# Block-sparse attention and two gated layers on one core: six weight pieces converted beside the first chunk's attention, small copies on GpSimd, loads for two groups

## The chip, the cores and the metric

One core of a Trainium2 chip runs the whole program. The time is the device time of one execution in microseconds; the median of several runs counts. The kernel before took 692.11 us (median of 3 runs, 690.9 to 693.22).

## What is computed

```python
def _attn_ref(q, k, v):                      # q, k, v: (2, 8, 768, 64) float32
    block, window = (32, 16)
    k_sum = k.reshape(B, H, nb, block, D).max(axis=3)
    v_sum = v.reshape(B, H, nb, block, D).mean(axis=3)
    scores_l = scale * np.matmul(q, k.transpose(0, 1, 3, 2))
    mask_l = np.abs(pos[:, None] - pos[None, :]) < window
    scores_s = scale * np.einsum('bhsd,bhnd->bhsn', q, k_sum) + np.log(block)
    scores_all = np.concatenate([np.where(mask_l, scores_l, -1e9), scores_s], axis=-1)
    a = softmax(scores_all)                  # with 1e-9 added to the sum
    return np.matmul(a, np.concatenate([v, v_sum], axis=2))

x = attention as (1536 tokens, 512)
x = ((x @ w_a) * (x @ w_b)) @ w_out          # 512 -> 1536 -> 512
h = x @ w_in                                 # 512 -> 2048
out = np.maximum(0.01 * h, h) @ w_out2       # 2048 -> 512
```

The weights come as float64. The kernel turns each into two float32r parts (high and low), does the same with activations, and makes each product from three float32r products.

## The kernel before

**Attention.** The 1536 tokens are cut into 3 chunks of 512. A chunk's attention is 8 groups; a group is one pair of heads and 256 queries in 4 windows of 64. In the first and third chunk two neighbouring groups share a head pair; in the second chunk, which lies across the two batches, no two do. For each group `load_q` (L130) and `load_vw` (L151) load queries and the windows of values, with one transfer for the queries and 4 to 6 for the windows; `q_prep` (L462) transposes queries on TensorE and ScalarE writes them, scaled, into a block-diagonal tile by four activations of 64x128 (L479, L480). `k_prep` (L436) transposes keys, takes the maximum over each 32 keys and copies the 24 block sums behind each window's keys (L455, on VectorE). `scores` (L483) multiplies, masks (L501, VectorE) and takes exponentials (L505, ScalarE). `normal` (L511) adds 1e-9 (L513) and takes the reciprocal (L514) on VectorE and multiplies on GpSimd (L515). `put_sums` (L181) copies the block sums of values into the group's window tile (L182, VectorE). `p_transpose` and `pv` finish the group; `pv` splits the result into two parts (L542, L543). `v_sums` (L390) adds values in blocks, mostly on GpSimd (L396).

**Weights.** 68 pieces of 512 KB are loaded by `stage` (L284, up to four ahead, three buffers) and converted by `convert` (L300) in seven steps: L316, L324, L329, L335, L341 and L349 on VectorE (the first, L316, together with L320 on ScalarE; L346 on ScalarE before L349). The results live in `W_EARLY` = 15 buffers, and in `W_LATE` = 9 more once the attention's memory is free, which is at the third chunk. The first chunk's products use 12 pieces, in the order a0 b0 a1 b1 a2 o0 b2 o1 a3 b3 o2 o3.

**Order.** `attention_ops` (L192) gives every step of group *i* a place 4*i* + offset; products (`PRODUCT`) are the steps with TensorE work. The first chunk's steps run in this order; after each product with a place over 9 (`PV`) one step of conversion is issued (`tick`, L360; L610), and at place 9 `first_weights` (L588) makes the first four pieces be converted if they aren't. `early` (L591) then feeds the first chunk's first four products (a0, b0, a1, b1) as its x tiles come. The later chunks' attention is cut into `micro` steps and issued between the matrix products of the chunk before at each call of `interleave` (L559), together with `pace["bg"]` = 3 steps of conversion. Then come the gated layer over 12 slices of 128 per chunk, in three rounds of four, and the second layer. All of this is the order of issue; the program's own scheduler, which works with a time model, then sets each engine's order and may pull a step forward into time that it holds to be idle. DMAs are all issued by SP.

Of the kernel before, what the change touches and what calls it, by code (L numbers as in the profile page):

```python
# [21 lines left out]
def kernel(  # L22
# [12 lines left out]
    nc = tc.nc  # L35
# [32 lines left out]
    W_EARLY, W_LATE = 15, 9  # L68
# [41 lines left out]
    vw_t = [keep.tile([P, 2, G, D], F32, tag=f"vw{i}", name=f"vw{i}") for i in range(2)]  # L110
# [9 lines left out]
    q_t, k_t, vb_t, vw_of = {}, {}, {}, {}  # L120
# [9 lines left out]
    def load_q(b, hp, g):  # L130
        t = q_p.tile([P, 2, GT // P, D], F32, tag="q", name="q")
        nc.sync.dma_start(
            out=t,
            in_=q[b, 2 * hp : 2 * hp + 2, g * GT : (g + 1) * GT].rearrange(
                "c (p n) d -> p c n d", p=P
            ),
        )
        q_t[b, hp, g] = t
# [12 lines left out]
    def load_vw(b, hp, g):  # L151

        t = vw_t[cnt["load"] % 2]
        cnt["load"] += 1

        def rows(o0, o1, w0, w1):
            if o0 < W < o1:
                rows(o0, W, w0, w1)
                rows(W, o1, w0, w1)
                return  # L160
            p0 = o0 + (KP if o0 >= W else 0)
            for c in range(2):
                src = v[b, 2 * hp + c, (g * G + w0) * W - WIN + o0, :]
                src = bass.AP(
                    tensor=src.tensor, offset=src.offset,
                    ap=[[D, o1 - o0], [W * D, w1 - w0], [1, D]],
                )
                nc.sync.dma_start(out=t[p0 : p0 + o1 - o0, c, w0:w1, :], in_=src)  # L168

        w0, w1 = int(g == 0), G - int(g == NGB - 1)  # L170
        if w0:
            rows(WIN, W, 0, 1)
        rows(0, W, w0, G)
        if w1 == G:
            rows(W, KL, 0, G)
        else:
            rows(W, W + WIN, 0, G)
            rows(W + WIN, KL, 0, w1)
        vw_of[b, hp, g] = t

    def put_sums(b, hp, g):  # L181
        nc.vector.tensor_copy(  # L182
            out=vw_of[b, hp, g][W : W + NB],
            in_=vs_t[b, 2 * hp // HV][:, 2 * hp % HV : 2 * hp % HV + 2, :]
            .unsqueeze(2)
            .to_broadcast([NB, 2, G, D]),
# [5 lines left out]
    def attention_ops():  # L192

        ops = []
        seen = set()
        for i, x in enumerate(sum(groups, [])):
            b, hp, g = x
            n = 4 * i

            def add(at, kind, f, *args):  # L200
                ops.append((n + at, kind, lambda: f(*args), i))
# [11 lines left out]
            add(-7, LOAD, load_q, *x)  # L213
# [3 lines left out]
            add(5, LOAD, load_vw, *x)  # L217
            add(7, SIDE, put_sums, *x)
# [217 lines left out]
    def k_prep(b, hp, g):  # L436
# [17 lines left out]
        if g == NGB - 1:  # L454
            nc.vector.tensor_copy(  # L455
# [6 lines left out]
    def q_prep(b, hp, g):  # L462
# [5 lines left out]
        for c in range(2):  # L468
            nc.tensor.transpose(
                ps[:, c * P : (c + 1) * P], q2[:, c].rearrange("p n d -> p (n d)"), ident  # L470
            )
        sc = -1.0 / math.sqrt(D)
        for c in range(2):

            dst = qbd[c * D : (c + 1) * D, :, c * W : (c + 1) * W].rearrange(
                "p w (o j) -> p w o j", j=2
            )
            src = ps[:, c * P : (c + 1) * P].rearrange("p (w o) -> p w o", w=G)
            nc.scalar.activation(out=dst[:, :, :, 0], in_=src[0:D], func=AF.Copy, scale=sc)  # L479
            nc.scalar.activation(out=dst[:, :, :, 1], in_=src[D:], func=AF.Copy, scale=sc)  # L480
# [30 lines left out]
    def normal(b, hp, g):  # L511
        pm, sm = st["pm", b, hp, g]
        nc.vector.tensor_scalar_add(sm, sm, 1.0e-9)  # L513
# [80 lines left out]

    n_first = len(groups[0])
# [6 lines left out]
    for i, x in enumerate(firsts):  # L602
        ops.append((PV, LOAD, lambda x=x: first_weights(*x), 0))
    ops.sort(key=lambda o: o[:2])
    rest = []
    for o in ops:
        if o[0] <= end or o[3] < n_first:
            o[2]()
            if o[1] == PRODUCT and o[0] > 0:
                tick(int(o[0] > PV))  # L610
# [82 lines left out]
    for n, (f, c) in enumerate(slices1):  # L693
        s, i = divmod(f, M1)
        if s == 0 and i == 0 and c + 1 < NC:
# [108 lines left out]
```

## Time and profile before

| | before |
|---|---|
| median of 3 runs | 692.11 us |
| the profiled execution | 693.21 us, its span 691.4 us |
| TensorE matmul busy | 650.4 us (94%) |
| VectorE busy | 421.7 us (61%) |
| ScalarE busy | 293.3 us (42%) |
| GpSimd busy | 50.7 us (7%) |
| mean granted TensorE clock | 0.968 |
| DMA | 53.43 MB, mean 77 GB/s |

A busy share is a mean over the span. The stages differ: attention fills the first 205 us or so, the matrix products the rest, so the shares are to be read stage by stage.

### The profile page before, as it was taken

How to read it: one execution, taken by the hardware profiler on the slowest of the kernel's cores; microseconds unless marked ns; L12 is line 12 of the kernel's file. 1: busy time of each engine (PE TensorE's matmuls, PEld its weight loads, DVE VectorE, ACT ScalarE, POOL GpSimd, SP SyncE). 2: the span in 40 equal slices, each digit the busy share in tenths (PEclk: the TensorE clock that was granted, in tenths of full speed). 3: DMA queues.
4: the chain of work that ended last, by engine and by line, in shares of the span. 5: the costliest groups of instructions: out<-in, count | busy, mean ns of one | idle time of the engine just before them, and what ended most of it. 6: DMA issues, size and time to landing. Idle time of an engine off the chain costs nothing.

```text
span 691.4 us, 9270 instructions
## 1 busy us (share of the span) xinstructions
PE 650.4 (94%) x3248; PEld 533.8 (77%) x3248; DVE 421.7 (61%) x978; ACT 293.3 (42%) x717; POOL 50.7 (7%) x79
## 2 busy tenths in 40 slices
PE   5697895999989999999999999999999999999997
PEld 4575784778768888888888888888888888888886
DVE  4999999443329999679924299943239432322423
ACT  6786566574545544244412255522235332222221
POOL 7324200110110000000000000000000000000000
PEclk9898997699989999999999999999999999999999
DMA  7976356220103444314410024210002000010101
GB/s 170 268 212 182 96 151 173 49 66 20 26 19 123 126 153 136 104 62 127 147 32 0 1 91 145 70 61 1 0 1 92 0 1 0 15 48 0 62 0 62
DMA packets 66862, 53.43 MB, mean 77 GB/s; under 512 B 34304, under 2 KB 60928, under 8 KB 66816
## 3 DMA queue, kind: packets, MB, share of 16 engines
q1 hardware_dynamic: 66816, 52.84, 25.6%
q8 instruction: 26, 0.43, 0.2%
q14 instruction: 20, 0.16, 0.1%
HBM read 49.68 MB, written 3.15 MB: 76 GB/s over the span
## 4 chain that ended last, share of the span: by engine, by line
PE 85%; DVE 8%; DMA 2%; SPq 2%; ACT 1%; issue 1%; DVEq 0%
PE ps_c L550 33%; PE ps_t L550 21%; PE ps_a L550 13%; PE ps_b L550 13%; PE ps_t L488 3%; DVE pm L501 1%; PE ps_t L534 1%; DMA vb<-in_v_dram 1%; DVE wc L335 1%; PE ps_t L523 1%; SPq L168 1%; ACT pm L505 1%; DVE vw L182 1%; DMA wst<-in_moe_w_a_dram 1%; DVE wc L324 1%
## 5 line engine op out<-in xcount | busy, mean ns | idle before, releaser
L550 PE MATMUL ps_c<-wsp,gs 128*128 128x512 f32 x576 | 139.6, 389 | 0.0
L550 PEld LDWEIGHTS ps_c<-wsp,gs 128*128 128x128 f32 x576 | 108.1, 188 | 22.5
L550 PE MATMUL ps_c<-gs,wsp 128*128 128x512 f32 x432 | 106.8, 392 | 0.0
L550 PEld LDWEIGHTS ps_c<-gs,wsp 128*128 128x128 f32 x432 | 80.3, 188 | 16.4
L550 PE MATMUL ps_t<-x,wsp 128*128 128x512 f32 x336 | 80.1, 394 | 0.0
L550 PEld LDWEIGHTS ps_t<-x,wsp 128*128 128x128 f32 x336 | 63.7, 190 | 13.4
L550 PE MATMUL ps_t<-ys,wsp 128*128 128x512 f32 x288 | 72.1, 389 | 0.0
L550 PE MATMUL ps_a<-x,wsp 128*128 128x512 f32 x252 | 69.7, 408 | 0.4 <-ACT x L542 0.2
L550 PE MATMUL ps_b<-x,wsp 128*128 128x512 f32 x252 | 66.5, 397 | 0.0
L550 PEld LDWEIGHTS ps_t<-ys,wsp 128*128 128x128 f32 x288 | 54.1, 188 | 11.2
L320 ACT ACTIVATE wc<-wst 128x512 f32<-128x512 f32 x68 | 46.0, 678 | 37.8 <-DVE wsp L349 37.2
L759 DVE SCALAR_TENSOR_TENSOR h<-h,ps_t 128x512 f32<-128x512 f32 x24 | 16.5, 686 | 67.6 <-ACT h L758 67.6
L550 PEld LDWEIGHTS ps_a<-x,wsp 128*128 128x128 f32 x252 | 47.3, 193 | 10.9 <-ACT x L542 1.7
L550 PEld LDWEIGHTS ps_b<-x,wsp 128*128 128x128 f32 x252 | 47.9, 191 | 9.5
L346 ACT CAST wsp<-wc 128x512 fp32r<-128x512 f32 x68 | 42.2, 622 | 29.4 <-DVE wc L341 27.6
L349 DVE TENSOR_TENSOR wsp<-wc,wsp 128x512 fp32r<-128x512 f32 x68 | 47.5, 699 | 10.5 <-ACT wsp L346 10.4
L335 DVE SCALAR_TENSOR_TENSOR wc<-wst,wc 128x512 int32<-128x512 int32 x68 | 48.9, 720 | 0.4
L341 DVE CUSTOM_DVE_ANT_0 wc<-wc,wr 128x1024 uint16<-128x1024 uint16 x68 | 48.5, 714 | 0.5
L505 ACT ACTIVATE pm<-pm,nb 128x128 f32<-128x128 f32 x96 | 37.7, 395 | 25.2 <-DVE nb L501 25.1
L571 DVE TENSOR_TENSOR gs<-h,gs 128x512 fp32r<-128x512 f32 x48 | 33.2, 691 | 24.7 <-ACT gs L570 24.5
L758 ACT COPY h<-ps_t 128x512 f32<-128x512 f32 x24 | 14.1, 587 | 72.4 <-PE ps_t L550 72.4
L570 ACT CAST gs<-h 128x512 fp32r<-128x512 f32 x48 | 29.8, 621 | 32.5 <-DVE h L759 29.4
(112 smaller groups left out, 800.9 us busy)
## 6 DMA issues: line engine op xcount, KB each, us to landing
wst<-in_moe_w_out_dram SPq DMA_DIRECT2D x28, 512.0 KB, 3.2
wst<-in_moe_w_in_dram SPq DMA_DIRECT2D x16, 512.0 KB, 3.7
wst<-in_moe_w_a_dram SPq DMA_DIRECT2D x12, 512.0 KB, 4.0
wst<-in_moe_w_b_dram SPq DMA_DIRECT2D x12, 512.0 KB, 3.9
k<-in_k_dram SPq DMA_DIRECT2D x16, 192.0 KB, 3.3
q<-in_q_dram SPq DMA_DIRECT2D x24, 128.0 KB, 2.8
vb<-in_v_dram SPq DMA_DIRECT2D x8, 384.0 KB, 5.5
out_dram<-acc SPq DMA_DIRECT2D x12, 256.0 KB, 2.1
```

The costliest lines, as they stand in the source:

```text
L320: nc.scalar.activation(out=t["c"].bitcast(F32), in_=hi_w.bitcast(F32), func=AF.Abs)
L335: nc.vector.scalar_tensor_tensor(out=t["c"], in0=hi_w, scalar=-0x40000000, in1=t["c"], op0=ALU.bitwise_and, op1=ALU.bitwise_or,)
L341: nc.vector.tensor_tensor(out=t["c"], in0=t["c"], in1=t["r"], op=ALU.add)
L346: nc.scalar.copy(out=t["w"][:, 0], in_=t["c"].bitcast(F32))
L349: nc.vector.tensor_tensor(out=t["w"][:, 1], in0=t["c"].bitcast(F32), in1=t["w"][:, 0].bitcast(F32), op=ALU.subtract,)
L488: nc.tensor.matmul(out=ps[:, w, :], lhsT=qbd[:, w, :], rhs=kts[:, (g * G + w) * SC : (g * G + w) * SC + P], start=True, stop=True,)
L505: nc.scalar.activation(out=pm[:, w, :], in_=pm[:, w, :], func=AF.Exp, scale=-1.0, bias=nb[:, w : w + 1], accum_out=sm[:, w : w + 1],)
L550: nc.tensor.matmul(out=ps, lhsT=w(a), rhs=x(b), start=first and j == 0, stop=last and j == 2)
L570: nc.scalar.copy(out=t[:, 0], in_=src)
L571: nc.vector.tensor_tensor(out=t[:, 1], in0=src, in1=t[:, 0].bitcast(F32), op=ALU.subtract)
L758: nc.scalar.copy(out=h, in_=ps)
L759: nc.vector.scalar_tensor_tensor(out=h, in0=h, scalar=0.01, in1=ps, op0=ALU.mult, op1=ALU.max)
```

## The change

Conversion: `W_EARLY` 14 and `W_LATE` 10. While the first chunk's attention is issued, two steps of conversion follow each product from the first on, until six pieces are begun; `first_weights` moves four places later. `pace["bg"]` is 4 in the first chunk, 1 in the second, 3 in the third, and 1.4 from the second round on. Loads: `load_q`, `load_vw` and `put_sums` work for *n* groups, two where the next group has the same heads and chunk; window tiles are twice as large, query tiles have two buffers for two groups each. Queries are laid out as keys are, so the block-diagonal tile takes two activations of 64x256 in place of four of 64x128. GpSimd takes the copies of block sums (L182, L455) and the addition of 1e-9 (L513).

```diff
-    W_EARLY, W_LATE = 15, 9
+    W_EARLY, W_LATE = 14, 10
-    vw_t = [keep.tile([P, 2, G, D], F32, tag=f"vw{i}", name=f"vw{i}") for i in range(2)]
+    vw_t = [keep.tile([P, 2, GC * G, D], F32, tag=f"vw{i}", name=f"vw{i}") for i in range(2)]
...
-    def load_q(b, hp, g):
-        t = q_p.tile([P, 2, GT // P, D], F32, tag="q", name="q")
-        nc.sync.dma_start(
-            out=t,
-            in_=q[b, 2 * hp : 2 * hp + 2, g * GT : (g + 1) * GT].rearrange(
-                "c (p n) d -> p c n d", p=P
-            ),
-        )
-        q_t[b, hp, g] = t
+    def load_q(b, hp, g, n):
+
+        t = q_p.tile([P, GC * GT // P, 2, D], F32, tag="q", name="q", bufs=2)
+        for c in range(2):
+            nc.sync.dma_start(
+                out=t[:, 0 : n * GT // P, c, :],
+                in_=q[b, 2 * hp + c, g * GT : (g + n) * GT].rearrange("(n p) d -> p n d", p=P),
+            )
+        for i in range(n):
+            q_t[b, hp, g + i] = t[:, i * GT // P : (i + 1) * GT // P]
...
-    def load_vw(b, hp, g):
+    def load_vw(b, hp, g, n):
...
+        nw = n * G
...
-        w0, w1 = int(g == 0), G - int(g == NGB - 1)
+        w0, w1 = int(g == 0), nw - int(g + n == NGB)
...
-    def put_sums(b, hp, g):
-        nc.vector.tensor_copy(
-            out=vw_of[b, hp, g][W : W + NB],
+    def put_sums(b, hp, g, n):
+        nc.gpsimd.tensor_copy(
+            out=vw_run[b, hp, g][W : W + NB],
...
-            .to_broadcast([NB, 2, G, D]),
+            .to_broadcast([NB, 2, n * G, D]),
...
-            add(-7, LOAD, load_q, *x)
...
-            add(5, LOAD, load_vw, *x)
-            add(7, SIDE, put_sums, *x)
+            run = (b, hp, g - 1) == prev
+            if not run:
+
+                n = 1 + int((b, hp, g + 1) in groups[i // len(groups[0])])
+                add(-7, LOAD, load_q, *x, n)
+                add(5, LOAD, load_vw, *x, n)
+                add(7, SIDE, put_sums, *x, n)
+            prev = x
...
-            nc.vector.tensor_copy(
+            nc.gpsimd.tensor_copy(
                 out=kts[:, 0:NW, W : W + NB],
...
         for c in range(2):
-            nc.tensor.transpose(
-                ps[:, c * P : (c + 1) * P], q2[:, c].rearrange("p n d -> p (n d)"), ident
-            )
...
-            nc.scalar.activation(out=dst[:, :, :, 0], in_=src[0:D], func=AF.Copy, scale=sc)
-            nc.scalar.activation(out=dst[:, :, :, 1], in_=src[D:], func=AF.Copy, scale=sc)
+
+            nc.scalar.activation(
+                out=qbd[c * D : (c + 1) * D, :, c * W : (c + 1) * W],
+                in_=ps[c * D : (c + 1) * D, :GT].rearrange("p (w o) -> p w o", w=G),
+                func=AF.Copy, scale=-1.0 / math.sqrt(D),
+            )
...
-        nc.vector.tensor_scalar_add(sm, sm, 1.0e-9)
+        nc.gpsimd.tensor_scalar_add(sm, sm, 1.0e-9)
...
+    N_FIRST = 6
...
-        ops.append((PV, LOAD, lambda x=x: first_weights(*x), 0))
+        ops.append((PV + 4, LOAD, lambda x=x: first_weights(*x), 0))
...
-            if o[1] == PRODUCT and o[0] > 0:
-                tick(int(o[0] > PV))
+            if o[1] == PRODUCT and o[0] > 0 and (bg or cnt["conv"] < N_FIRST):
+                tick(2)
...
         s, i = divmod(f, M1)
+        if i == 0:
+            pace["bg"] = {(0, 0): 4, (0, 1): 1, (0, 2): 3}.get((s, c), 1.4)
```

## Rows read from the trace of the kernel before

**Rows 1.** Stages: busy us (instructions) per engine, granted clock, DMA share, GB/s.

```profile
0.00:20.00 20.00, 11.85 (x55) 10.26 (x56) 9.72 (x48) 12.21 (x47) 13.31 (x48) 1.00 0.75 189
20.00:120.00 100.00, 77.25 (x531) 61.00 (x532) 96.86 (x275) 69.95 (x233) 25.80 (x20) 0.88 0.64 178
120.00:147.00 27.00, 24.20 (x178) 18.85 (x176) 12.48 (x57) 17.54 (x70) 5.18 (x5) 0.76 0.22 54
147.00:205.00 58.00, 54.31 (x366) 44.37 (x365) 20.02 (x84) 27.13 (x94) 6.40 (x7) 0.94 0.12 29
205.00:691.00 486.00, 482.78 (x2130) 399.37 (x2128) 282.64 (x514) 166.48 (x276) 0.00 (x0) 1.00 0.18 59
```

**Rows 2.** The page's slices: VectorE's busy tenths in 40 equal slices.

```profile
DVE  4999999443329999679924299943239432322423
```

**Rows 3.** Chain of waits, around 50 us: start, length, what.

```profile
50.39 1.66 DVE wc L335
52.05 1.15 DVE sm L513
```

**Rows 4.** Timeline of GpSimd at the same time: start, length, instruction.

```profile
50.04 3.13 POOL L396 TENSOR_TENSOR vb<-vb,vb 96x512 f32<-96x512 f32 x2
```

**Rows 5.** The three moved lines, whole run: ns min/median/max, first and last start.

```profile
L182 DVE COPY vw<-vs x24: 410/419/1372, 18.7 to 194.2; 24x512 f32<-24x512 f32 x24
L455 DVE COPY kts<-ks x8: 297/366/1369, 6.9 to 124.1; 128x288 f32<-128x288 f32 x8
L513 DVE TENSOR_SCALAR sm<-sm x24: 148/168/1225, 15.6 to 195.5; 128x4 f32<-128x4 f32 x24
```

**Rows 6.** VectorE's lines from 205 us on: count, busy us, mean ns, idle before.

```profile
L335 DVE SCALAR_TENSOR_TENSOR wc<-wst,wc 128x512 int32<-128x512 int32 x51 | 34.9, 686 | 0.2
L329 DVE TENSOR_SCALAR wc<-wc 128x512 int32<-128x512 int32 x51 | 21.5, 421 | 0.1
```

**Rows 7.** VectorE's lines from 20 to 120 us, same columns.

```profile
L335 DVE SCALAR_TENSOR_TENSOR wc<-wst,wc 128x512 int32<-128x512 int32 x17 | 14.0, 823 | 0.2
L341 DVE CUSTOM_DVE_ANT_0 wc<-wc,wr 128x1024 uint16<-128x1024 uint16 x17 | 13.6, 798 | 0.1
L349 DVE TENSOR_TENSOR wsp<-wc,wsp 128x512 fp32r<-128x512 f32 x15 | 11.2, 746 | 0.4 <-ACT wsp L346 0.4
L329 DVE TENSOR_SCALAR wc<-wc 128x512 int32<-128x512 int32 x17 | 8.4, 492 | 0.0
L316 DVE TENSOR_SCALAR wr<-wst 128x512 int32<-128x512 uint32 x19 | 7.9, 417 | 1.0 <-DMA wst<-in_moe_w_a_dram 0.9
...
L324 DVE TENSOR_SCALAR wc<-wc 128x512 f32<-128x512 f32 x17 | 7.8, 456 | 0.0
L182 DVE COPY vw<-vs 24x512 f32<-24x512 f32 x10 | 5.8, 587 | 0.5 <-PE ps_c L534 0.2
...
L513 DVE TENSOR_SCALAR sm<-sm 128x4 f32<-128x4 f32 x11 | 3.9, 352 | 0.0
...
L455 DVE COPY kts<-ks 128x288 f32<-128x288 f32 x5 | 3.4, 681 | 0.0
```

**Rows 8.** GpSimd: two lines over the run (min/median/max ns), one instruction by time.

```profile
L226 POOL MEMSET vw<- x2: 524/524/525, 0.7 to 1.2; 128x512 f32 x2
...
L515 POOL TENSOR_TENSOR pm<-pm,sm x24: 1038/1040/1307, 16.3 to 196.1; 128x512 f32<-128x512 f32 x24
...
8.84 0.11 POOL L256 MEMSET negm_last<- 128x16 f32 x1
```

**Rows 9.** Chain of waits at the first conversion.

```profile
16.18 4.28 DMA wst<-in_moe_w_a_dram
```

**Rows 10.** Chain of waits at the end of the third chunk's attention.

```profile
197.94 1.64 DMA vw<-in_v_dram
```

**Rows 11.** DMA issues over the run: count, KB each, median us to landing.

```profile
k<-in_k_dram SPq DMA_DIRECT2D x16, 192.0 KB, 3.3
q<-in_q_dram SPq DMA_DIRECT2D x24, 128.0 KB, 2.8
```

More of the change, by code (lines that the diff above doesn't have):

```diff
@@ L119 @@
     pace = {"micro": 0.0, "bg": 3}
-    q_t, k_t, vb_t, vw_of = {}, {}, {}, {}
+    q_t, k_t, vb_t, vw_of, vw_run = {}, {}, {}, {}, {}
     def load_k(b, hp):
@@ L168, in rows @@
                 nc.sync.dma_start(out=t[p0 : p0 + o1 - o0, c, w0:w1, :], in_=src)
-        w0, w1 = int(g == 0), G - int(g == NGB - 1)
+        w0, w1 = int(g == 0), nw - int(g + n == NGB)
         if w0:
             rows(WIN, W, 0, 1)
-        rows(0, W, w0, G)
-        if w1 == G:
-            rows(W, KL, 0, G)
+        rows(0, W, w0, nw)
+        if w1 == nw:
+            rows(W, KL, 0, nw)
         else:
-            rows(W, W + WIN, 0, G)
+            rows(W, W + WIN, 0, nw)
             rows(W + WIN, KL, 0, w1)
-        vw_of[b, hp, g] = t
-    def put_sums(b, hp, g):
-        nc.vector.tensor_copy(
-            out=vw_of[b, hp, g][W : W + NB],
+        for i in range(n):
+            vw_of[b, hp, g + i] = t[:, :, i * G : (i + 1) * G, :]
+        vw_run[b, hp, g] = t[:, :, 0:nw, :]
+    def put_sums(b, hp, g, n):
+        nc.gpsimd.tensor_copy(
+            out=vw_run[b, hp, g][W : W + NB],
             in_=vs_t[b, 2 * hp // HV][:, 2 * hp % HV : 2 * hp % HV + 2, :]
             .unsqueeze(2)
-            .to_broadcast([NB, 2, G, D]),
+            .to_broadcast([NB, 2, n * G, D]),
         )
@@ L195, in attention_ops @@
         seen = set()
+        prev = None
         for i, x in enumerate(sum(groups, [])):
             b, hp, g = x
-            n = 4 * i
             def add(at, kind, f, *args):
-                ops.append((n + at, kind, lambda: f(*args), i))
+                ops.append((4 * i + at, kind, lambda: f(*args), i))
             vi, r = divmod(2 * hp, HV)
@@ L467, in q_prep @@
         ps = at_bank()
+        for i in range(GT // P):
+            nc.tensor.transpose(
+                ps[:, i * P : (i + 1) * P], q2[:, i].rearrange("p c d -> p (c d)"), ident
+            )
         for c in range(2):
-            nc.tensor.transpose(
-                ps[:, c * P : (c + 1) * P], q2[:, c].rearrange("p n d -> p (n d)"), ident
-            )
[L472 to L476, printed above, removed]
-            )
-            src = ps[:, c * P : (c + 1) * P].rearrange("p (w o) -> p w o", w=G)
-            nc.scalar.activation(out=dst[:, :, :, 0], in_=src[0:D], func=AF.Copy, scale=sc)
-            nc.scalar.activation(out=dst[:, :, :, 1], in_=src[D:], func=AF.Copy, scale=sc)
+            nc.scalar.activation(
+                out=qbd[c * D : (c + 1) * D, :, c * W : (c + 1) * W],
+                in_=ps[c * D : (c + 1) * D, :GT].rearrange("p (w o) -> p w o", w=G),
+                func=AF.Copy, scale=-1.0 / math.sqrt(D),
+            )
         st["qk", b, hp, g] = qbd
```

## The prediction

> **What bounds the kernel now.** I read the views from coarse to fine. The page's engine table puts TensorE at 94% of the span and so says little. Cutting the span into stages [rows 1] says more: from 205 us on TensorE is busy for 482.8 of 486 us at a granted clock of 1.00 (the 2.4 GHz level), all of it expert matrix products that the change doesn't touch. Nothing is to be had there; what the change can win or lose lies in the first 205 us, and shifts the rest as a block.
>
> In those 205 us there are three stretches. In the first 20 us VectorE is busy for 9.72 us only. From 20 to 120 us it is busy for 96.86 of 100 us, while TensorE has 77.25, ScalarE 69.95 and the DMA engines 64% [rows 1]; the row of VectorE's slices shows the same block of nines [rows 2]. This is a VectorE-bound stretch: first-chunk attention, weight conversion and half of the second chunk's attention share one engine. From 120 to 205 us TensorE is nearly full again (24.20 of 27 and 54.31 of 58 us), but at mean clocks of 0.76 and 0.94, so the clock stood at its 1.2 GHz level for part of them.
>
> Inside the VectorE stretch the chain of waits shows a second thing: instructions that take much longer than they should. A 128x4 addition stands there with 1.15 us and a join of weights with 1.66 us [rows 3], while GpSimd runs two additions from 50.04 to 53.17 us [rows 4]. The usual times are 168 ns for that addition [rows 5] and 686 ns for that join [rows 6]. So a GpSimd instruction holds up VectorE instructions that work in SBUF.
>
> **The change part by part.** All sums go against the profiled execution, 693.2 us (span 691.4 and 1.8 around it); it lies 1.1 us above the median of 692.1.
>
> *Three kinds of small instructions leave VectorE for GpSimd.* In the stretch they are 10 copies of value sums (L182, 5.8 us), 11 additions of 1e-9 (L513, 3.9) and 5 copies of key sums (L455, 3.4) [rows 7]. At their undisturbed medians of 419, 168 and 366 ns [rows 5] that is 4.2 + 1.85 + 1.8 = 7.9 us of work; the other 5.3 us were waiting for GpSimd, and will fall on the next SBUF instruction instead. So 7.9 us leave VectorE. What comes back is the hold-up by the new GpSimd work. Its price per us: in the stretch five of the conversion's six instructions are longer than in the GpSimd-free part after 205 us [rows 6, 7] (L341 and L349 differ from L335, and L324 from L329, by under 1 ns there): 17 x 137, 17 x 112, 15 x 60, 17 x 71 and 17 x 35 ns, 6.9 us; with the 5.3 above 12.2 us, for 25.8 us of GpSimd [rows 1], 0.47 us per us.
>
> No row shows GpSimd doing such copies. Its clear of 128x512 takes 524 ns and its two-input product of 128x512 takes 1040 [rows 8]; a copy reads one stream, so I take the middle, 0.75 us for 512 columns (ends 0.52 and 1.04) and 1.5 us for the 1024 of two groups. In the stretch that makes about three double copies and three single ones (6.8 us), five key copies of 288 columns (about 0.45 each, 2.2), and eleven tiny additions, for which the 0.11 us clear of 16 columns [rows 8] is nearest (0.15 each, 1.6): 10.6 us, ends 7.3 and 15. At 0.47 this returns 5.0 us. Net **-2.9 us**; ends -7.9 (no hold-up) and +7.1 (15 us, all of it held up).
>
> *A rule of the Trainium skill speaks against this part.* What the rows show is above: 1.15 us for a 168 ns addition under a GpSimd instruction [rows 3, 5]. The Trainium skill, "GPSIMD Engine Reference", Key points, says that GpSimd shares its SBUF interfaces with VectorE and contends with VectorE instructions in a two-port mode or with two SBUF inputs; the trace agrees, with 1.15 us for 0.168. Its section Engine selection has one-input GpSimd work at roughly line rate; by the page's 1.2 GHz a double copy would be about 0.85 us (an estimate), and the net of this part nearer -5.
>
> *Fewer conversions in the stretch.* The early pool goes from 15 to 14 pieces, and 15 conversions finish in the stretch [rows 7]. One conversion is 417 + 456 + 492 + 823 + 798 + 746 ns = 3.7 us of VectorE [rows 7]. That one piece moves past 205 us, where VectorE has 203 us free [rows 1]: **-3.7 us**. Two further pieces have five of their six steps in the stretch although their room comes later (17 against 15 in [rows 7]); the program's scheduler pulls them forward into what it thinks is idle time. I leave them where they are (0; -6 if they now stay out).
>
> *Conversion starts earlier.* Ticks now run from the first products on instead of from the first group's P.V product. Before, the first weight's transfer takes 4.28 us from 16.18 us on and VectorE waits for it [rows 9]. Moved ahead, three 512 KB transfers pass the first value windows and keys on SP's queue. Those have some us of slack, since VectorE, not they, is late afterwards; the DMA engines are at 75% in the first 20 us [rows 1]. VectorE idles for 10.3 of these 20 us; about one piece should fit: **-4 us** (0 to -7).
>
> *Key-sum copy behind the masks.* The first such copy starts at 6.9 us on VectorE [rows 5]. On GpSimd it queues behind the mask set-up, whose last instruction starts at 8.84 [rows 8], and the first scores and exponentials wait for it: **+1.5 us** (0 to +2). Later normalisations and copies stand in one GpSimd queue too; a product that waits for a reciprocal holds the copies behind it, which is in the ends above.
>
> *Loads for two groups.* They halve the value-window transfers in the first and third chunk and make buffers free sooner. At the end of the third chunk's attention there is a wait of this kind: the last group's window lands until 199.6 us [rows 10], since its buffer comes free only when the group two before it is done. TensorE idles 3.7 us in that stage and its clock of 0.94 over 58 us costs up to 3.5 more [rows 1]. I take **-4 us** (0 to -7). Queries now come in 256-byte runs, as the keys already do; 192 KB of keys land 3.3 us after issue and 128 KB of queries after 2.8 [rows 11], so I price that at nothing. Two activations of twice the columns in place of four relieve ScalarE, which isn't the bound: nothing, as long as VectorE covers it.
>
> *Clock.* If TensorE is starved less before 120 us, part of the 0.76 in the 27 us behind it (6.5 us) comes back: **-2 us** (0 to -6).
>
> *Pace later.* 1.4 steps at each of some six interleave points per slice is 8.4 steps, 1.2 pieces per slice, against 12 pieces for 12 slices. Enough, and VectorE has room: nothing. If a piece came late, TensorE would wait for about one conversion, 3.7 us.
>
> Sum: -2.9 - 3.7 - 4 + 1.5 - 4 - 2 = -15.1. 693.2 - 15.1 = 678.1, and against the median 1.1 less: **677 us**.
>
> **The rivals.** *Slower, by the shared port.* GpSimd instructions cost their upper ends (15 us more in the stretch) and each of their microseconds stops VectorE, since this engine is always in an SBUF instruction there: +15 - 7.9 = +7.1; the earlier weights compete with keys and values and give nothing, +2 at the start, -3.7 for the piece, 0 in the third chunk: +5.4, about 697. It decides where hold-up per us times new GpSimd time passes 11.6 us. For it: [rows 3]. Against it: at the measured 0.47 it would need 25 us of new GpSimd time.
>
> *The wait moves to the weights.* Only six of the twelve pieces that the first chunk's products use are ready when its attention ends. At one piece per 6.7 us (15 in 100 us, [rows 7]) the twelfth came at about 100 us; if attention ends near 66 us and the six others keep that rhythm, it comes at 106, and TensorE stands in front of the products. That eats -2.9, -3.7, -4 and the clock; the third chunk's -4 and +1.5 remain: 690. For it: by the same rhythm the kernel before had eight pieces at 77 us, six are fewer. Against it: VectorE has less else to do then.
>
> *More than that.* Pieces 13 and 14 and the two begun ones really move to 120 us and later, where VectorE is busy for 12.48 of 27 and 20.02 of 58 us [rows 1]: 2 x 3.7 + 2 x 3.0 = 13.4 more, and 2 of clock: 662.
>
> *Not what it says.* The scheduler may pull the seventh and later conversions beside the first chunk anyway, as it did with pieces 16 and 17. Then VectorE's sum stays as I have it, and so does the time; it is part of the forecast.
>
> **How the numbers follow.** Forecast (668 to 686) 0.45; more (662) 0.17; weights late (690) 0.20; port (697) 0.18. A measurement of this kernel tells about 0.3%, 2.1 us, from no change. Faster by that, below 690.0: 0.45 + 0.17 + half of 0.20, 0.72; the other half within it, with a little of the port case, 0.12; slower 0.16. For 8 in 10 I reach from 661 to 695: this leaves the far half of the large gain and the far half of the port case outside.
>
> **What would show it.** Right: the end of the VectorE block at 105 to 110 us in place of 120, no idle TensorE before the last P.V product of the third chunk, and everything after it moved as a block. The port shows as conversions and additions stretched to a GpSimd instruction's end, and as GpSimd copies of over 1 us. Late weights show as TensorE waiting for a conversion's last subtraction before the first chunk's third or fourth slice. Wrong altogether if TensorE idles after 205 us.

## The result, and the profile after

The kernel after took 701.6 us (median of 4 runs) beside 692.04 us for the kernel before: a ratio of 1.0134 [1.0093, 1.0175]. It is slower, where 677 us and a gain had been forecast, and it lies outside the range given. The profiled execution took 703.6 us, its span 701.5.

The stages of the kernel after, with the columns of [rows 1] (busy us and instructions of TensorE, its weight loads, VectorE, ScalarE, GpSimd; granted clock, DMA share, GB/s):

```profile
0.00:20.00 20.00, 11.32 (x50) 9.60 (x50) 10.36 (x48) 10.71 (x38) 15.05 (x50) 1.00 0.96 233
20.00:120.00 100.00, 75.94 (x463) 60.05 (x462) 83.11 (x212) 56.66 (x178) 43.01 (x43) 0.85 0.57 153
120.00:147.00 27.00, 20.03 (x153) 15.63 (x151) 9.80 (x46) 14.67 (x57) 6.15 (x11) 0.75 0.29 65
147.00:205.00 58.00, 54.09 (x383) 43.48 (x378) 18.29 (x88) 31.75 (x107) 14.70 (x22) 1.00 0.19 43
205.00:230.00 25.00, 23.56 (x149) 19.04 (x148) 16.19 (x40) 12.73 (x29) 1.93 (x3) 1.00 0.19 61
230.00:701.00 471.00, 467.84 (x2064) 387.20 (x2062) 271.99 (x493) 159.01 (x263) 0.00 (x0) 1.00 0.18 59
```

From 230 us on the matrix products run as before, at 1.00 and 99% busy, so the loss lies ahead of them. In the 20 to 120 us stretch VectorE is busy for 83.11 us in place of 96.86 [rows 1]: it did get the relief that the change was to bring, and more of it (13.8 us) than the prediction's sum has for this stretch (2.9, 3.7 and 4). TensorE has not gained from it (75.94 against 77.25 us busy). GpSimd went from 25.80 to 43.01 us.

VectorE's slices show where the relief went; the row answers to [rows 2]:

```profile
DVE  4799993332337999759984187983239532232423
```

The block of nines is shorter: it ends at the sixth slice, near 105 us, where before it reached the seventh, near 120. That was forecast as the sign of success, and here it is no success: the attention results come later. ScalarE copies each group's P.V result out of PSUM, so its eighth copy marks the end of the first chunk's attention, its 24th the end of all attention:

| | eighth result, us | 24th result, us | span, us | conversions finished before the eighth |
|---|---|---|---|---|
| before | 69.1 | 200.4 | 691.4 | 6 |
| after | 87.7 | 212.1 | 701.5 | 12 |

The row of that eighth copy after (start, length, what):

```profile
87.74 0.35 ACT L549 CAST x<-ps_c 128x256 fp32r<-128x256 f32 x1
```

18.6 us are lost by then; 5.8 come back in the second chunk, for which only two of the 14 early conversions are left, and 1.1 in the third. That the conversions are the reason isn't shown: e13 below, with seven left, makes up as much there. In both kernels the span ends 489 to 491 us after the 24th result. So a late eighth result is not lost time one for one; the ratios decide.

### The profile page after: what moved, and what is told of

It is laid out like the page before. It is cut to its first block, busy times and chain, and to the rows that moved or that the text cites. A ratio compares the mean times of both kernels' runs of the same rounds, so it can differ in the third digit from the quotient of the medians.

```text
span 701.5 us, 9146 instructions
## 1 busy us (share of the span) xinstructions
PE 652.8 (93%) x3248; PEld 535.0 (76%) x3248; DVE 409.7 (58%) x922; ACT 285.5 (41%) x669; POOL 80.8 (12%) x127
## 4 chain that ended last, share of the span: by engine, by line
PE 84%; DVE 6%; ACT 4%; issue 2%; POOL 2%; DMA 1%; SPq 1%; POOLq 0%; ACTq 0%; DVEq 0%
PE ps_c L557 33%; PE ps_t L557 20%; PE ps_a L557 13%; PE ps_b L557 13%; PE ps_t L495 3%; ACT pm L512 2%; PE ps_t L530 1%; DVE pm L508 1%; PE ps_t L541 1%; DMA vb<-in_v_dram 1%; POOL pm L522 1%; DVE wc L333 1%; DVE wc L344 1%; DVE v L415 1%; DVE wsp L358 1%
## 5 line engine op out<-in xcount | busy, mean ns | idle before, releaser
L557 PEld LDWEIGHTS ps_c<-wsp,gs 128*128 128x128 f32 x576 | 108.2, 188 | 22.4
L557 PEld LDWEIGHTS ps_c<-gs,wsp 128*128 128x128 f32 x432 | 80.7, 188 | 16.6
L358 DVE TENSOR_TENSOR wsp<-wc,wsp 128x512 fp32r<-128x512 f32 x68 | 50.1, 741 | 13.2 <-ACT wsp L355 13.1
L350 DVE CUSTOM_DVE_ANT_0 wc<-wc,wr 128x1024 uint16<-128x1024 uint16 x68 | 48.7, 720 | 0.4
```

Of the source, the lines that this page charges most:

```text
L350: nc.vector.tensor_tensor(out=t["c"], in0=t["c"], in1=t["r"], op=ALU.add)
L358: nc.vector.tensor_tensor(out=t["w"][:, 1], in0=t["c"].bitcast(F32), in1=t["w"][:, 0].bitcast(F32), op=ALU.subtract,)
L557: nc.tensor.matmul(out=ps, lhsT=w(a), rhs=x(b), start=first and j == 0, stop=last and j == 2)
```

## The experiments

Ratios are to the kernel before, run beside each kernel. `issue_after(x)` in a diff sets an instruction behind x in its own engine's order and adds no other wait. "V" stands for the value-sum copies (L182 before, L186 after), "K" for the key-sum copies (L455, L464), "A" for the additions of 1e-9 (L513, L520).

### One part undone, or one part alone

**e1: the kernel after with V, K and A back on VectorE.**

```diff
-        nc.gpsimd.tensor_copy(
+        nc.vector.tensor_copy(
             out=vw_run[b, hp, g][W : W + NB],
...
-            nc.gpsimd.tensor_copy(
+            nc.vector.tensor_copy(
                 out=kts[:, 0:NW, W : W + NB],
...
-        nc.gpsimd.tensor_scalar_add(sm, sm, 1.0e-9)
+        nc.vector.tensor_scalar_add(sm, sm, 1.0e-9)
```

> The changed kernel with its three moves to GpSimd undone (both copies of sums and the addition of 1e-9 back on VectorE); conversion, pace and loads stay changed. Theory F (the fill): with slower steps on GpSimd the program's scheduler holds VectorE to be idle in the first chunk's attention and fills it with conversions pulled forward; in VectorE's order 12 of 14 conversions stand before the eighth group's result in the changed kernel, 7 of 15 in the one before, 8 of 14 in this one. At 3.7 us each that is four less than in the changed kernel, 15 us at the first chunk's end, about half of it left at the end: 690 to 694, the eighth result near 72 us. Theory P (the port): only the hold-up by GpSimd goes, about 3 us: 698. Theory L (the loads of two groups and the early weights crowd the first 20 us of DMA): 700.

Measured 0.9951 [0.9924, 0.9977]; eighth result at 69.5 us.

**e2: the kernel after with the conversion's old places and pace.**

```diff
-            if o[1] == PRODUCT and o[0] > 0 and (bg or cnt["conv"] < N_FIRST):
-                tick(2)
+            if o[1] == PRODUCT and o[0] > 0:
+                tick(int(o[0] > PV))
...
-        ops.append((PV + 4, LOAD, lambda x=x: first_weights(*x), 0))
+        ops.append((PV, LOAD, lambda x=x: first_weights(*x), 0))
...
-            pace["bg"] = {(0, 0): 4, (0, 1): 1, (0, 2): 3}.get((s, c), 1.4)
+            pace["bg"] = 3
```

> The changed kernel with the pace of conversion as before (one step per product behind the ninth place, first weights at the ninth place, three steps per interleave point); GpSimd moves and loads stay changed. Theory C (the new pace, two steps from the first product on, is what brings conversions in front of attention): back to 692. Theory F: in VectorE's order 11 conversions still stand before the eighth result, so the pace is not the cause: 698 to 702. Theory P: 701.

Measured 1.009 [1.0062, 1.0118]; eighth result at 87.3 us, ten conversions before it.

**e3: the kernel after with loads and value sums for one group.**

```diff
-            run = (b, hp, g - 1) == prev
+            run = False
...
-                n = 1 + int((b, hp, g + 1) in groups[i // len(groups[0])])
+                n = 1
```

> The changed kernel, but loads and copies of value sums for one group each (window and query tiles keep their new size). Theory L: back to 692 to 694. Theory F: 10 conversions in place of 12 stand before the eighth result: 695 to 699. Theory P: as many microseconds on GpSimd or a little more: 701 to 703.

Measured 1.0082 [1.0049, 1.0114]; eighth result at 80.4 us.

**e4: the kernel before with V, K and A on GpSimd** (e1's edit the other way round).

> The kernel before with the three moves to GpSimd alone. Theory F: 11 conversions in place of 7 stand before the eighth result, 15 us at the end of the first chunk, about half of it left: 697 to 702. Theory P: the hold-up by some 15 us of new GpSimd time less the 8 us that leave VectorE: 690 to 695. Theory L and theory C: 688 to 692, since neither loads nor pace are touched.

Measured 1.0112 [1.0059, 1.0165]; eighth result at 79.7 us. e1 and e4 put the loss on the three moves to GpSimd: they cost 1.1% in the kernel before and 1.8% in the kernel after, and the rest of the change gains 0.5%. Undoing the conversion or the loads leaves most of the loss.

### Which of the three moves

**e7: the kernel after with V alone back on VectorE** (the first of e1's three edits).

> The changed kernel with the copies of value sums alone back on VectorE; key sums and the addition of 1e-9 stay on GpSimd. 8 conversions in place of 12 stand before the eighth result without any queueing by hand. Theory F: 689 to 694, as with all three moves undone. Theory G: the addition in the chain from exponentials to product stays on GpSimd, with its three changes of engine per group; 695 to 699.

Measured 0.9904 [0.9878, 0.993]; eighth result at 66.2 us, seven conversions before it. It beats both kernels (687.64 us beside 694.25 for the kernel before).

**e14: the kernel before with V alone on GpSimd.**

> The kernel before with only the copies of value sums on GpSimd; eight conversions stand before the eighth result, one more than before. Theory QF: little is out of order, ratio 1.000 to 1.005. Theory C: the whole loss of the three GpSimd moves in the kernel before, ratio 1.009 to 1.013.

Measured 1.0015 [0.9991, 1.004]; eighth result at 72.1 us.

**e15: the kernel after with K and A back on VectorE**, V alone on GpSimd.

> The kernel after with the key-sum copies and the additions of 1e-9 back on VectorE; only the value sums stay on GpSimd. Ten conversions stand before the eighth result (twelve after, eight with the value sums back on VectorE). If the time follows the number of conversions that the order sets before the eighth result: eighth result near 80 us, ratio 1.003 to 1.009. If it takes the three moves together (an addition, a product and copies that wait for each other in GpSimd's queue), the additions on VectorE take the loss away: ratio 0.994 to 0.999.

Measured 0.9989 [0.9954, 1.0025]; eighth result at 76.2 us, nine conversions before it. The ratio is the one forecast for the three moves together.

**e16: the kernel before with V and A on GpSimd.**

> The kernel before with the value-sum copies and the additions of 1e-9 on GpSimd, the key sums left on VectorE. Nine conversions stand before the eighth result (seven before, eight with the value sums alone, eleven with all three). If the time follows that number: between the 1.0015 of the value sums alone and the 1.011 of all three, 1.004 to 1.008. If copies and additions in one queue are what costs, whatever the order on VectorE: 1.009 or more.

Measured 1.0105 [1.0059, 1.0151]; eighth result at 76.5 us, nine conversions before it. This is the whole loss of e4.

**e17: the kernel after with A alone back on VectorE. e18: with K alone back.**

> The kernel after with the additions of 1e-9 alone back on VectorE; value sums and key sums stay on GpSimd. Eleven conversions stand before the eighth result. If the loss takes additions and value sums together in GpSimd's queue: ratio 0.994 to 1.001, eighth result at 75 us or earlier. If it follows the number of conversions ahead of the eighth result, whatever is on GpSimd: ratio 1.007 to 1.012, eighth result at 80 us or later.

> The kernel after with the key-sum copies alone back on VectorE; value sums and additions stay on GpSimd. Eleven conversions stand before the eighth result. Both theories expect a slow version, ratio 1.007 to 1.014; if it is at 1.000 or below, the key sums are needed for the loss, and neither holds.

Measured 1.0009 [0.9987, 1.003] for e17 and 1.0052 [1.0022, 1.0082] for e18; ten conversions before the eighth result in both, at 81.4 and 83.9 us. e17's ratio fits the first theory and its eighth result the second; e18 is below the range that both gave. So the number of conversions ahead of the eighth result does not set the time by itself: e17 and e4 both have ten, and lie a percent apart.

The kernel after with each set of moves on GpSimd:

| on GpSimd | without V | with V | what V adds |
|---|---|---|---|
| neither K nor A | 0.9951 (e1) | 0.9989 (e15) | 0.4% |
| K | not run | 1.0009 (e17) | - |
| A | not run | 1.0052 (e18) | - |
| K and A | 0.9904 (e7) | 1.0134 (after) | 2.3% |

No single move loses much: K and A alone gain 0.5%, V alone costs 0.4% (the intervals overlap in both), and together they cost 1.8%, so 1.9% (13 us) belongs to the combination.

### Order or queue

Two causes were to be told apart. **By the order on VectorE:** with a fuller GpSimd the program's order sets more conversions ahead of the first chunk's results. **By the queue:** GpSimd takes its instructions in order (e5's rows below show an addition of 0.22 us that is ready at 71.2 us and starts at 74.25), a group's normalisation passes through it twice (addition, product), and what stands between holds the group up.

The first is plain in VectorE's conversion lines up to the eighth result (count, busy us, mean ns, idle before). In the kernel after, up to 87.7 us:

```profile
L358 DVE TENSOR_TENSOR wsp<-wc,wsp 128x512 fp32r<-128x512 f32 x12 | 11.3, 943 | 1.9 <-ACT wsp L355 1.9
L350 DVE CUSTOM_DVE_ANT_0 wc<-wc,wr 128x1024 uint16<-128x1024 uint16 x13 | 11.2, 865 | 0.0
L344 DVE SCALAR_TENSOR_TENSOR wc<-wst,wc 128x512 int32<-128x512 int32 x13 | 10.0, 775 | 0.1
L333 DVE TENSOR_SCALAR wc<-wc 128x512 f32<-128x512 f32 x13 | 8.9, 687 | 0.4 <-ACT wc L329 0.2
L325 DVE TENSOR_SCALAR wr<-wst 128x512 int32<-128x512 uint32 x14 | 8.4, 599 | 0.0
L338 DVE TENSOR_SCALAR wc<-wc 128x512 int32<-128x512 int32 x13 | 6.4, 501 | 0.1
```

In e7 (V on VectorE), up to 66.2 us:

```profile
L358 DVE TENSOR_TENSOR wsp<-wc,wsp 128x512 fp32r<-128x512 f32 x7 | 7.5, 1081 | 0.1
L350 DVE CUSTOM_DVE_ANT_0 wc<-wc,wr 128x1024 uint16<-128x1024 uint16 x8 | 7.0, 885 | 0.0
L344 DVE SCALAR_TENSOR_TENSOR wc<-wst,wc 128x512 int32<-128x512 int32 x8 | 5.4, 682 | 0.1
L186 DVE COPY vw<-vs 24x1024 f32<-24x1024 f32 (+1 forms) x6 | 5.1, 879 | 0.1
L333 DVE TENSOR_SCALAR wc<-wc 128x512 f32<-128x512 f32 x9 | 5.1, 561 | 0.6 <-ACT wc L329 0.6
L325 DVE TENSOR_SCALAR wr<-wst 128x512 int32<-128x512 uint32 x9 | 4.2, 465 | 0.1
L338 DVE TENSOR_SCALAR wc<-wc 128x512 int32<-128x512 int32 x8 | 3.6, 457 | 0.0
```

The six conversion lines sum to 56.2 us after and 32.8 in e7: 23.4 us more, against 21.5 us by which the eighth result is later. At the undisturbed 686 and 421 ns [rows 6] the 78 instructions after are 42.9 us and the 49 of e7 26.7, so 16.2 of the 23.4 are more instructions and 7.2 are longer ones. That says what VectorE did in the time; whether the order caused the delay, or only filled it, is for the next runs.

**e5: the kernel after with each conversion held behind the first chunk's latest result.**

```diff
...
-            nc.vector.tensor_scalar(
-                out=t["r"], in0=lo_w.bitcast(U32), scalar1=2.0**-29, scalar2=None, op0=ALU.mult
-            )
+            with tc.issue_after(latest["pv"].ins) if latest else ExitStack():
+                nc.vector.tensor_scalar(
+                    out=t["r"], in0=lo_w.bitcast(U32), scalar1=2.0**-29, scalar2=None,
+                    op0=ALU.mult,
+                )
...
-        nc.vector.tensor_tensor(
+        ins = nc.vector.tensor_tensor(
             out=x[:, 1], in0=ps[:, :GT], in1=x[:, 0].bitcast(F32), op=ALU.subtract
         )
+        if c == 0:
+            latest["pv"] = ins
```

> The changed kernel with one line more: the first VectorE step of each conversion is queued behind the latest group's result of the first chunk that was issued before it, so that the scheduler can't pull the seventh and later conversions in front of the first chunk's attention. GpSimd moves, loads and pace stay. In VectorE's order 7 in place of 12 conversions stand before the eighth result, as in the kernel before. Theory F (the fill): 5 x 3.7 = 18 us come back at the eighth result (68 to 74 us in place of 88), 10 at the end: 689 to 693. Theory G (waits in the GpSimd queue itself, and its hold-up of VectorE, make the first chunk slow, whatever conversions do): the eighth result stays near 85 us, 698 to 702.

Measured 1.0062 [1.0038, 1.0086]; seven conversions before the eighth result, at 80.7 us. Fewer conversions stand ahead, and most of the delay stayed. But the holding sets in late, since a conversion issued before the first result is held behind nothing: ahead of the third result VectorE starts 32 conversion steps here, 33 in the kernel after and 22 in e7, and the fifth result comes at 63.6 us here and after, at 52.3 in e7. From the fifth result to the eighth, where the holding acts, it takes 17.1 us in place of 24.1 (e7 13.9). So e5 tests the order on VectorE for the last three groups alone. There VectorE now waits instead; its longest wait of the first chunk is for an addition of 1e-9. VectorE's row in this run's timeline (start, length, what, in brackets the idle time before and who ended it):

```profile
74.51 0.18 DVE L524 RECIPROCAL sm<-sm 128x4 f32<-128x4 f32 x1 [4.48 <-POOL sm L523]
```

And GpSimd's rows in the same timeline, from 71 to 77 us:

```profile
71.67 2.50 POOL L408 TENSOR_TENSOR vb<-vb,vb 96x512 f32<-96x512 f32 x2 [2.89 <-DMA vb<-in_v_dram]
74.25 0.22 POOL L523 TENSOR_SCALAR sm<-sm 128x4 f32<-128x4 f32 x1
74.55 1.28 POOL L408 TENSOR_TENSOR vb<-vb 96x512 f32<-96x512 f32 x1
75.80 1.04 POOL L525 TENSOR_TENSOR pm<-pm,sm 128x512 f32<-128x512 f32 x1
```

The group's exponentials were done at 71.2 us. Its addition of 0.22 us stood in GpSimd's queue behind 2.50 us of value additions for a later chunk; its reciprocal, and VectorE behind it, waited; and the product then stood behind another value addition.

**e6: e4 with the same holding. e8: e1 with it. e11: e7 with it.**

> The kernel before with the three moves to GpSimd (701.9 us alone) and the same queueing of conversions: 8 in place of 11 stand before the eighth result. Theory F: 3 x 3.7 = 11 us back at the eighth result, which came at 79.7, so near 69; 692 to 695. Theory G: 699 to 702.

> The changed kernel without GpSimd moves (689.0 us) and with the queueing of conversions: 7 in place of 8 stand before the eighth result. Theory F: a gain of about one conversion, 3.7 us there and half of it at the end: 685 to 689. Theory G: no change, 689.

> The version with only the value sums back on VectorE, with the first step of each conversion queued behind the latest result of the first chunk's attention that was issued before it: seven conversions in place of eight stand before the eighth result. If what is left of the first chunk's time is set by conversions that stand too early (F), it gains another 2 to 4 us: ratio 0.985 to 0.988. If not, the ratio stays at 0.990 within 0.002.

Measured 1.0068 [1.0045, 1.0092] for e6, 0.9918 [0.9891, 0.9946] for e8, 0.9905 [0.987, 0.9939] for e11; eighth results at 77.4, 68.1 and 66.2 us. Holding brings 0.7% to the kernel after, beyond the intervals; the 0.4% for e4 and 0.3% for e1 are within them, and e7 gains nothing.

**e9: the kernel after with V queued behind the latest product. e12: e9 and e5 together.**

```diff
...
-        nc.gpsimd.tensor_copy(
-            out=vw_run[b, hp, g][W : W + NB],
...
+        with tc.issue_after(latest["mult"].ins):
+            nc.gpsimd.tensor_copy(
+                out=vw_run[b, hp, g][W : W + NB],
...
-        nc.gpsimd.tensor_tensor(
+        latest["mult"] = nc.gpsimd.tensor_tensor(
             out=pm, in0=pm, in1=sm.unsqueeze(2).to_broadcast([P, G, P]), op=ALU.mult
```

> The kernel after with one edit: a value-sum copy on GpSimd is queued only behind the latest product of the normalisation that was issued before it, so that additions and products stand ahead of copies in GpSimd's queue. The work and its engines stay as they are after the change; ten conversions stand before the first chunk's eighth result in VectorE's order. Theory Q (the copies stand too early in GpSimd's in-order queue and hold up the additions and products behind them): the first chunk's eighth result comes near 70 us and the ratio to before is 0.990 to 0.998 (687 to 692). Theory D (a result waits for its value sums, because on GpSimd they come late, whatever their order): the eighth result stays at 80 us or later, ratio 1.005 or more. Theory F (more conversions beside the first chunk): ratio about 1.003.

> The kernel after with both orders mended at once: the value-sum copies on GpSimd queued behind the latest product issued before them, and each conversion's first step on VectorE queued behind the latest result of the first chunk; seven conversions stand before the eighth result. One mended alone left 1.006 (conversions held) and 1.016 (copies behind the product). Theory QF (two orders, each enough to make the first chunk late, the copies themselves cheap): ratio 0.990 to 0.998. Theory C (the copies cost on the chip whatever stands where, since group after group waits for GpSimd): VectorE idles again before the eighth result, ratio 1.004 or more.

Measured 1.0156 [1.0121, 1.0191] and 1.0217 [1.0172, 1.0263]; eighth results at 85.2 and 80.7 us. e9 is as slow as the kernel after within the intervals, e12 slower. These two don't test the queue cleanly. A copy now stands behind products of other groups than its own; in the third chunk the last eight results take 61 us in both runs, 55 in the kernel after. Why they do isn't shown: no long wait for a copy stands in e9's trace. That the copies need only a better place is refuted for this place, and open for others.

**e10: e7 with four idle GpSimd copies, of V's size, in the first chunk. e13: e10 with the conversions held.** The copies add work that nobody reads.

```diff
...
+        if b * S + g * GT < T:
+            nc.gpsimd.tensor_copy(
+                out=spare[0:NB, :, 0 : n * G, :],
+                in_=ident[0:NB].rearrange("p (c d) -> p c d", c=2)
...
```

> The version with only the value sums back on VectorE (0.990 of before), with four GpSimd copies of the same size added in the first chunk; they read a constant, nobody reads what they write, and they wait for nothing. Theory Q: the copies displace additions and products all the same, ratio 1.002 to 1.012. Theory D: nobody waits for them, so only their hold-up of VectorE is left, about 4 us of GpSimd time at 0.47, 2 us: ratio 0.990 to 0.994. Theory F: eleven conversions stand before the eighth result as in the slow versions, ratio 1.005 or more.

> The version with the value sums on VectorE and four idle GpSimd copies (1.010 of before), with each conversion's first step on VectorE queued behind the latest result of the first chunk; seven conversions stand before the eighth result in place of eleven. Theory QF: only the copies' place in GpSimd's queue and their hold-up are left, ratio 0.992 to 0.998. Theory C: 1.006 or more.

Measured 1.01 [1.0063, 1.0137] for e10 and 1.0001 [0.9968, 1.0035] for e13, where the same versions without the idle copies have 0.9904 (e7) and 0.9905 (e11). Eighth results at 87.1 and 79.5 us; e10's ratio fits two of its theories, e13's falls between its two. Nobody reads what the copies write: 4.8 to 5.1 us of GpSimd copies cost 2.0% (14 us) by being there. Seven of these 14 us go when the conversions are held, so at least that much is VectorE's order. The other seven remain, with a later start of GpSimd's chain. Rows of GpSimd's timeline in e13:

```profile
8.25 1.03 POOL L195 COPY spare<-ident 24x1024 f32<-24x1024 f32 x1
10.21 0.42 POOL L475 COPY kts<-ks 128x288 f32<-128x288 f32 x1
14.29 1.23 POOL L195 COPY spare<-ident 24x1024 f32<-24x1024 f32 x1
15.91 1.25 POOL L416 TENSOR_TENSOR vb<-vb 96x512 f32<-96x512 f32 x1
27.00 1.40 POOL L533 TENSOR_TENSOR pm<-pm,sm 128x512 f32<-128x512 f32 x1 [0.34 <-DVE sm L532]
```

And of e11, the same key-sum copy and the same first product:

```profile
9.23 0.42 POOL L467 COPY kts<-ks 128x288 f32<-128x288 f32 x1
18.16 1.80 POOL L525 TENSOR_TENSOR pm<-pm,sm 128x512 f32<-128x512 f32 x1 [2.14 <-DVE sm L524]
```

An idle copy of 1.03 us puts the first key-sum copy 1.0 us later, but the first group's product starts at 27.00 in place of 18.16 us. What lies between is seen on VectorE. Its rows in e13: two conversion steps, the first mask, the first reciprocal.

```profile
13.92 0.72 DVE L335 TENSOR_SCALAR wr<-wst 128x512 int32<-128x512 uint32 x1 [2.64 <-DMA wst<-in_moe_w_a_dram]
14.62 2.82 DVE L344 TENSOR_SCALAR wc<-wc 128x512 f32<-128x512 f32 x1
...
18.76 0.28 DVE L519 CUSTOM_DVE_ANT_0 pm<-ps_c,negm_first 128x128 f32<-128x128 f32 x1
...
26.76 0.16 DVE L532 RECIPROCAL sm<-sm 128x4 f32<-128x4 f32 x1
```

And in e11, the first mask, the first conversion step, the first reciprocal:

```profile
11.92 0.29 DVE L511 CUSTOM_DVE_ANT_0 pm<-ps_c,negm_first 128x128 f32<-128x128 f32 x1 [1.75 <-PE ps_c L498]
...
13.45 0.78 DVE L327 TENSOR_SCALAR wr<-wst 128x512 int32<-128x512 uint32 x1
...
17.91 0.17 DVE L524 RECIPROCAL sm<-sm 128x4 f32<-128x4 f32 x1
```

In e13 five conversion steps stand ahead of the first mask and 14 ahead of the first reciprocal, in e11 none and three; the addition had ended at 21.04, so the reciprocal waited 5.7 us on VectorE. The first scores start at 13.02 in place of 9.71 us, since TensorE's order puts two transposes of queries ahead of them, which wait 2.2 us for their load. So the orders of VectorE and TensorE are not mended in e13 before its first result, and of the 13.3 us by which its eighth result is later than e11's, 10.4 are there by the fourth. The seven us that remain can't be put down to GpSimd's queue alone.

### The same two things in the kernel after

Group 6's normalisation (the sixth of the first chunk), in the kernel's timeline, first GpSimd's rows:

```profile
55.47 2.68 POOL L186 COPY vw<-vs 24x1024 f32<-24x1024 f32 x2 [1.81 <-ACT vs L439]
58.24 0.27 POOL L520 TENSOR_SCALAR sm<-sm 128x4 f32<-128x4 f32 x1
66.37 2.57 POOL L522 TENSOR_TENSOR pm<-pm,sm 128x512 f32<-128x512 f32 x2 [1.50 <-DVE sm L521]
```

And VectorE's rows up to the reciprocal:

```profile
64.65 0.76 DVE L350 CUSTOM_DVE_ANT_0 wc<-wc,wr 128x1024 uint16<-128x1024 uint16 x1
65.33 0.41 DVE L325 TENSOR_SCALAR wr<-wst 128x512 int32<-128x512 uint32 x1
65.71 0.43 DVE L333 TENSOR_SCALAR wc<-wc 128x512 f32<-128x512 f32 x1
66.05 0.23 DVE L521 RECIPROCAL sm<-sm 128x4 f32<-128x4 f32 x2
```

Its exponentials end at 55.7 us. The addition waits 2.5 us behind two value-sum copies in GpSimd's queue. It is ready at 58.5, but the reciprocal runs at 66.05, as a pair with the next group's, and VectorE is not idle ahead of it: eleven conversion steps start in between, which its order puts first (the last three are among the rows above). From the end of the exponentials to the reciprocal the first chunk's groups take 4.5 us on average after, 1.7 in e7, 2.6 before. Against e7 the wait for the addition to start, in GpSimd's queue, grows from 0.4 to 1.1 us per group, and the wait from the addition's end to the reciprocal, on VectorE, from 1.0 to 3.1. These waits overlap from group to group and are not shares of the time, but the larger one is VectorE's.

TensorE starves meanwhile. From 60 to 80 us it is busy for 11.19 of 20 us, with the clock at its 1.2 GHz level throughout, where the kernel before has 15.88 us at a mean clock of 0.88 and e7 15.83 at 1.00 (the stage's row after, columns as above):

```profile
60.00:80.00 20.00, 11.19 (x64) 8.84 (x65) 19.39 (x43) 10.35 (x30) 9.93 (x9) 0.50 0.48 148
```

## Why the prediction was wrong

**The step that failed is the first one: "a VectorE-bound stretch".** VectorE was busy for 97% of it [rows 1], but a good part of that is conversion, which is not urgent: the 14 pieces are finished by 98.6 us after and by 108.2 us before for their first 14, and the attention is late all the same. What sets the end of the first chunk is when each group's steps get their turn, on a chain that now runs through ScalarE, GpSimd, VectorE and GpSimd again. The prediction counted microseconds on VectorE; 13.8 of them did go, and the time rose by 1.3%.

**GpSimd moves, -2.9 (ends -7.9 and +7.1).** Measured +7.8 us in the kernel before (e4) and +12.7 in the kernel after (1.0134 against e1's 0.9951). Both medians are outside the ends (e4's interval, 4.1 to 11.4 us, reaches 7.1), though the terms of the sum were close: the moved work took 13.7 us of GpSimd in the stretch, where 10.6 was taken with 15 as the end. The sizes: a copy of 1024 columns 1.03 us at its median (1.5 taken), of 512 0.60 (0.75), of 288 0.42 (0.45), an addition 0.22 (0.15). The hold-up: the conversion lines of 20 to 120 us sum to 63.8 us where 686 and 421 ns would make 48.7, so 15.1 us for 43.0 of GpSimd; by the prediction's working it was 12.2 for 25.8, and 5.0 more for new work. It grew by 2.9. GpSimd's products became longer in turn, 1.50 us on average in the stretch in place of 1.15, which had no term. Above all, what had no term is the place of these instructions: the prediction had "a product that waits for a reciprocal holds the copies behind it" as being "in the ends above", and it was neither in the ends nor in that direction only, since copies also hold additions and products, and new work on GpSimd changes the order on VectorE.

**One conversion fewer, -3.7; conversion earlier, -4; loads, -4; clock, -2.** All that is left of the change without GpSimd is -0.5% (e1), 3.4 us [1.6 to 5.3], where these terms sum to -13.7. Earlier conversion was had as forecast: 4.0 us of conversion steps run in the first 20 us, none before. Beside the GpSimd moves it doesn't pay: e2, with the old places and pace, is 0.4% faster than the kernel after, within the intervals; without them it wasn't run. The piece moved later saved VectorE time that bounded nothing, but no run moves it back alone. Loads for two groups: from the 16th to the 24th result e1 and e7 take 53.8 us, the kernel before 56.0, so 2.2 us of the 4; the wait of [rows 10] is not in their chain. In the kernel after one-group loads were the faster ones (e3, by 0.5%, the intervals overlap). The clock of the 27 us from 120 us on did not come back: 0.75 after, 0.76 before.

**Key sums behind the masks, +1.5.** The first scores start 1.6 us later (9.7 against 8.1 us). Right, and no loss in the end: e7 has it, too.

**The rival "port"** gave +5.4 and named the wrong mechanism. GpSimd copies of over 1 us and conversions stretched in a row are there, but the hold-up is no larger than forecast (15.1 us where 12.2 and 5.0 were). Its threshold of 11.6 us leaves out the +2 of the same rival; with it, it is 9.6. **"Not what it says"** came true: twelve pieces are done in the first chunk, not six. It was put at nothing, as costing no time, and that is the second step that failed: half of what the idle copies cost in e10 goes when the conversions are held, and 0.7% of the kernel after. Late weights and the large gain did not occur.

**What stays open.** Shown: the loss is in the first chunk; it needs V on GpSimd beside A (and K); copies without any reader bring a loss of the same size, and half of it goes when conversions are held. Not shown: how the rest divides between GpSimd's queue and the new order on VectorE and TensorE. The holding leaves the order ahead of the first results as it was (e5, e13), and no run kept all engines' orders as in e7. For the change itself holding the conversions brings 0.7% back of 2.3%. That the scheduler's time model holds GpSimd's queue to be longer, and fills the time with conversions, is argued from the orders, not shown.

## What to carry to other kernels

An engine that is 97% busy is a bound only if its work is urgent: take the filler out of its busy time first, then follow one group from engine to engine. Moving small instructions to an engine that already stands in that chain can cost far more than their microseconds (here 5 us of copies that nobody reads cost 14), by their place in its queue and by the orders that they change on other engines; try each move alone and in pairs (here K and A gain 0.5% without V, and lose with it). And read the new order of every engine, step by step and group by group: seven whole conversions stood ahead of the eighth result in e5, e7, e11 and e13 alike, and their orders still differed.

## What the hardware showed

The hold-up between VectorE and GpSimd works both ways. The first product of the kernel after takes 3.60 us, where its median is 1.04. GpSimd's row in the timeline:

```profile
17.82 3.60 POOL L522 TENSOR_TENSOR pm<-pm,sm 128x512 f32<-128x512 f32 x1 [2.16 <-DVE sm L521]
```

And VectorE's rows at the same time:

```profile
17.97 0.76 DVE L338 TENSOR_SCALAR wc<-wc 128x512 int32<-128x512 int32 x2
18.64 1.29 DVE L344 SCALAR_TENSOR_TENSOR wc<-wst,wc 128x512 int32<-128x512 int32 x2
19.84 0.69 DVE L350 CUSTOM_DVE_ANT_0 wc<-wc,wr 128x1024 uint16<-128x1024 uint16 x1
```

VectorE's five steps have their usual lengths, and the GpSimd instruction ends 0.9 us after the last of them, at 21.42 us. The Trainium skill, "SBUF — State Buffer", section Who interferes with whom, says that of a GpSimd instruction and a VectorE instruction in a two-port mode whichever issues first keeps the shared pair of ports for its whole instruction and the other one blocks; the trace agrees that either can be the loser ([rows 3] and [rows 4] show VectorE as it). Here the product took 2.6 us more than its median, under a train of five VectorE instructions; that the train held it is read from the times, not tested.

GpSimd copies of one input are cheap in columns: 0.42, 0.60 and 1.03 us for 288, 512 and 1024 columns, 0.8 ns a column and some 0.2 us besides.
